# A gated mix of a spectral filter and a GEGLU network, forward and backward: the forward transform by six column classes, and another order at the start of pass two

## The chip, the core and the metric

One core of a Trainium2 chip runs the whole kernel in one launch. The time is the device time of an execution in microseconds (us). Engine names are those of the profile: PE is TensorE (PEld its weight loads), DVE is VectorE, ACT is ScalarE, POOL is GpSimd, SP is SyncE, which issues most DMAs. A name with a q (ACTq, POOLq) is an engine's own DMA issuing.

## The reference

With S = 2048 rows, D = 576 columns and F = 4608, everything in bfloat16 at the borders:

```python
g = sigmoid((x * gate_w).sum(-1, keepdims=True))
a = irfft2(rfft2(x) * (w_r + 1j * w_i))          # spectral filter, 2048 x 576
b = (gelu(x @ w_gate) * (x @ w_up)) @ w_down     # GEGLU network
out = g * a + (1 - g) * b
```

The kernel returns `out` and, for a given `grad_out`, the gradients of x, w_r, w_i, w_gate, w_up, w_down and gate_w (the B branch's own x enters as a constant, and both branches read A's x). So there are two forward transforms, one of x and one of g times grad_out, and two inverse ones: one gives a, the other the branch's part of the gradient of x.

## The kernel before

All matrix work is on TensorE in bfloat16, and the kernel has two passes.

**Pass one** (0 to about 919 us) loops over 18 column groups g of 256 columns of F, and in each over four stages m of 512 rows: 72 stages, counted by `pr`, some 12 us each. A stage computes `H_mm` (matmuls z, L490 and L495, and xy, L499 and L506), the activation and its derivative on ScalarE (`H_act`, L525 to L528, `H_da`, L518) and VectorE (`H_ew1`, L533 to L537; `H_ew2`, L553 to L574), and the weight gradients of the group before (`W_units`: dw_down at L618, dw_gate and dw_up at L636, a tail at L650). ScalarE or VectorE evicts those (L587) into staging tiles, which GpSimd's DMA queue stores (L628, L643). The tile q, written by ScalarE at L525, is read by VectorE through L570 of the same stage.

Between the W jobs of a stage stand pieces of the spectral work, the list `fft`. `want(pr)` says how many are to be done by stage pr: the first nine values are in `FIRST`, the rest grow evenly. `fft_next` emits the next piece; a piece marked `noslot` goes along with the next one and takes no slot. First come the forward transforms, 16 row tiles of x and then 16 of grad_out, from 73.7 to 356 us. A row tile has two pieces:

- `u1(t)`: matmuls from the transposed input (`xT`, `dOT`) along the columns, which are split in four classes of 128 columns and a tail of 64. Six matmuls: four of 146 columns out with the table `D4` (L679), two of 292 with the tail table `D4t` (L682). ScalarE evicts the result to Y (for grad_out with the scale `gs32`, which is g times a constant).
- `u2(t)`: two matmuls of 292 columns (L697) with the row table `Rt[t]`, an eviction on ScalarE (L701, 128x584 elements), and five VectorE operations (L702 to L709) that make the 289 frequencies out of 73; then a store to DRAM.

PSUM for the results of both pieces comes from the pool of z, which has one buffer. After 356 us come the pieces in the middle (transform along the rows, products with the spectral weights, gradients of w_r and w_i) to about 806 us.

**Pass two** (from about 919 us) multiplies the stored activations by the weights again: a list of jobs g0, g1, b0, ..., whose matmuls stand at L1194. The inverse transforms run between them as pieces: `z_piece` (six matmuls of 128 columns, L1244, evicted by ScalarE at L1246) and `d_piece` (six of 96 columns, L1254), released by a counter, `ticks`, which every block of twelve matmuls moves on. The inverse already works by six classes of columns: `fold` (L1221 to L1237, 17 VectorE operations) makes them out of the loaded frequencies Vp (`load_p`, L1210, on ScalarE's DMA queue). Ahead of the jobs `build_RT` (VectorE L215 to L221, ScalarE's sines at L222) and `build_I` (VectorE L181 to L204, a sine at L203) make the inverse's tables. `spread_gw` broadcasts gate_w over the partitions by two matmuls into two accumulators and two VectorE copies (L1186). Accumulators come from one pool in turn, so each use waits until the use some tiles before has been read. In every job some loads of the transposed w_up (`load_wuT`, nine pairs) go to SyncE's queue.

Instructions are issued on each engine in program order, and the program order is that in which the Python code calls them.

Of the kernel before, what the change touches and what calls it, by code (L numbers as in the profile page):

```python
# [9 lines left out]
ACT = mybir.ActivationFunctionType  # L10
# [28 lines left out]
QF = 73  # L39
# [23 lines left out]
def iotas(nc, res, unit):  # L63
    tb = Tables()
    G, V = nc.gpsimd, nc.vector
    kw = dict(allow_small_or_imprecise_dtypes=True)
    tb.halfpi = res.tile([P, 1], F32, name="halfpi")
    V.memset(tb.halfpi[:], math.pi / 2)
    tb.pi = res.tile([P, 1], F32, name="pi")
    V.memset(tb.pi[:], math.pi * EPS_SCALE)  # L70
    tb.warm = res.tile([P, 1], F32, name="warm")
    nc.scalar.activation(tb.warm[:], tb.halfpi[:], ACT.Sin)
    tb.lrow = unit([QF], F32, name="lrow")
    G.iota(tb.lrow[:], pattern=[[1, QF]], base=0, channel_multiplier=0, **kw)
    tb.dcol = res.tile([P, 5], F32, name="dcol")
    G.iota(tb.dcol[:, 0:4], pattern=[[1, 4]], base=0, channel_multiplier=4, **kw)
    for r in (LO, HI):
        G.iota(tb.dcol[r, 4:5], pattern=[[0, 1]], base=512, channel_multiplier=1, **kw)
    tb.dn = res.tile([P, 5], F32, name="dn")
    V.tensor_scalar(tb.dn[:], tb.dcol[:], 1.0 / D, None, op0=ALU.mult)  # L80
    tb.late = []
    tb.Dt = []
    tb.Rt = []
    return tb


def iotas_R(nc, tb, res, unit, kscr):
# [16 lines left out]
    r4_i = res.tile([P, 1], I32, name="r4_i")  # L104
    tb.r4 = res.tile([P, 5], F32, name="r4_f")

    def parity():
        V.tensor_single_scalar(par_i[:], tb.qcol_i[:], 1, op=ALU.bitwise_and)
        V.tensor_copy(tb.par[:, 1:2], par_i[:])
        V.tensor_scalar(tb.par[:, 0:1], tb.par[:, 1:2], -1.0, 1.0, op0=ALU.mult, op1=ALU.add)  # L110
        V.tensor_scalar(tb.kadd[:, 0, 1:2], tb.par[:, 1:2], float(S // 2), float(S // 4), op0=ALU.mult, op1=ALU.add)
        kr = unit([3, P], F32, name="kr")
        G.tensor_scalar(kr[0:1, 0, :], kk[0:1, 0, :], 16.0, None, op0=ALU.mult)
        G.memset(kr[0:1, 0, 1:2], float(S // 2))
        G.tensor_copy(kr[0:1, 1:3, :], kk[0:1])
        nc.sync.dma_start(kscr[:].rearrange("(o k) m -> o k m", o=1), kr[0:1])
        nc.sync.dma_start(tb.kc[:], kscr[:].rearrange("k m -> m k"))
        V.tensor_single_scalar(r4_i[:], tb.qcol_i[:], 3, op=ALU.bitwise_and)
        V.tensor_copy(tb.r4[:, 4:5], r4_i[:])
        for r in range(4):  # L120
            G.tensor_scalar(tb.r4[:, r:r + 1], tb.r4[:, 4:5], float(r), None, op0=ALU.is_equal)
# [8 lines left out]
def build_D(nc, tb, unit, c0, n, w):  # L130

    V, G = nc.vector, nc.gpsimd
    step = 2.0 * math.pi / D
    TS = (G if c0 else V).tensor_scalar
    X = unit([n, w], F32, name="XD")
    y = unit([n, w], F32, name="yD")
    for c in range(n):
        TS(y[:, c, :], tb.lrow[:, 0:w], tb.dn[:, c0 + c:c0 + c + 1], MAGIC, op0=ALU.mult, op1=ALU.add)
    TS(y[:], y[:], -MAGIC, -float(D), op0=ALU.add, op1=ALU.mult)
    o = unit([n, 2, w], name="Dt")  # L140

    def angles():
        for c in range(n):
            V.scalar_tensor_tensor(X[:, c, :], tb.lrow[:, 0:w], tb.dcol[:, c0 + c:c0 + c + 1], y[:, c, :],
                                   op0=ALU.mult, op1=ALU.add)
        V.scalar_tensor_tensor(y[:], X[:], -1.0, X[:], op0=ALU.mult, op1=ALU.max)

    def sines():
        if c0 == 0:
            v = o[:].rearrange("p (o r) c l -> p o (r c) l", o=2)  # L150
            co, si = v[:, :, 0:4:3, :], v[:, :, 1:3, :]
            yv, Xv = (t[:].rearrange("p (o r) l -> p o r l", o=2) for t in (y, X))
        else:
            co, si, yv, Xv = o[:, :, 0, :], o[:, :, 1, :], y[:], X[:]
        nc.scalar.activation(co, yv, ACT.Sin, bias=tb.halfpi[:], scale=-step)
        nc.scalar.activation(si, Xv, ACT.Sin, scale=-step * EPS_SCALE)
        if c0 == 0:
            tb.D4 = o

    def tails():  # L160
        tl = tb.D4t = unit([2, 2, 4, w], name="Dt")
        G.memset(tl[HI, 0], 0.0)
        G.memset(tl[LO, 1], 0.0)
        for k, h in enumerate((LO, HI)):
            for r in range(4):
                for c in range(2):
                    b = 3 * c if r % 2 == 0 else 2 - c
                    G.tensor_scalar(tl[h, k, r // 2, b], o[h, 0, c], tb.r4[h, r:r + 1], None, op0=ALU.mult)
    return angles, sines, tails


# [153 lines left out]
def kernel(  # L325
# [101 lines left out]
    gs32 = res.tile([P, T], F32, name="gs32")  # L427
# [243 lines left out]
    def fwd_units(src, dst, scale, ps=pftile):  # L671
        ys = {}

        def u1(t):
            def f():
                yps = ps()
                for o in range(2):
                    for r, bs in ((2 * o, slice(0, 4, 3)), (2 * o + 1, slice(1, 3))):
                        nc.tensor.matmul(yps[:, o, 0:4 * QF].rearrange("p (b l) -> p b l", b=4)[:, bs, :], lhsT=src[:, r, t, :],  # L679
                                         rhs=tb.D4[:, r], start=(r % 2 == 0), stop=False)  # L680
                for o in range(2):
                    nc.tensor.matmul(yps[:, o, 0:4 * QF], lhsT=src[:, 4, t, :],  # L682
                                     rhs=tb.D4t[:, t % 2, o].rearrange("p b l -> p (b l)"), start=False, stop=True)
                ys[t] = unit([2, 4 * QF], name="Y")
                if scale is None:
                    nc.scalar.copy(ys[t][:], yps[:, :, 0:4 * QF])
                else:
                    nc.scalar.activation(ys[t][:], yps[:, :, 0:4 * QF], ACT.Copy, scale=scale[:, t:t + 1])
            return f

        def u2(t):
            def f():
                Y = ys.pop(t)
                R = tb.Rt[t]
                vps = ps()
                for o in range(2):
                    nc.tensor.matmul(vps[:, o, 0:4 * QF], lhsT=R, rhs=Y[:, o], start=True, stop=True)  # L697
                Vt = half([2, DF], name="Vt")
                ve = unit([8, QF], F32, name="ve")
                M = unit([2, 2, 2, QF], F32, name="vm")  # L700
                nc.scalar.copy(ve[:].rearrange("p (o b) l -> p o (b l)", o=2), vps[:, :, 0:4 * QF])  # L701
                V.tensor_tensor(M[:, 0].rearrange("p u v l -> p v u l"), ve[:, 0:4].rearrange("p (v u) l -> p v u l", u=2),  # L702
                                ve[:, 4:8].rearrange("p (v u) l -> p v u l", u=2), op=ALU.add)
                V.tensor_tensor(M[:, 1, 0], ve[:, 0:2], ve[:, 4:6], op=ALU.subtract)
                V.tensor_tensor(M[:, 1, 1], ve[:, 6:2:-3], ve[:, 2:8:5], op=ALU.subtract)
                up = Vt[:, :, 0:DF - 1].rearrange("p c (k l) -> p k c l", k=2)[:, :, :, 0:QF]
                dn = Vt[:, :, DF - 1:0:-1].rearrange("p c (k l) -> p k c l", k=2)[:, :, :, 0:QF - 1]
                V.tensor_tensor(up, M[:, :, :, 0], M[:, :, :, 1], op=ALU.add)
                V.tensor_tensor(dn, M[:, :, :, 0, 0:QF - 1], M[:, :, :, 1, 0:QF - 1], op=ALU.subtract)  # L709
                LD.dma_start(dst[:, t], Vt[:])  # L710
            return f
        return [u1(t) for t in range(T)], [u2(t) for t in range(T)]

# [160 lines left out]
    D0 = build_D(nc, tb, unit, 0, 4, QF)  # L874
    D0[0]()
# [3 lines left out]
    D4 = build_D(nc, tb, unit, 4, 1, QF)  # L879
    for f in titems(wdn, wts[0][1][:].rearrange("p k (c m) -> p k c m", c=2), 0, (phtile, pgtile, phtile), (VC, AC, VC), n=2):  # L880
        f()
    D0[1]()
# [3 lines left out]
    D4[0]()  # L886
    D4[1]()
# [10 lines left out]
    fg = zipped(*fwd_units(xT, scr_x, None)) + zipped(*fwd_units(dOT, scr_g, gs32))  # L898
# [28 lines left out]
    FIRST = (0, 0, 0, 0, 0, 0, 1, 4, 7)  # L927
# [37 lines left out]
    for g in range(NG):  # L965
# [3 lines left out]
        for m in range(NPR):  # L969
# [15 lines left out]
            if g == 0:  # L985
# [37 lines left out]
                elif m == 1:  # L1023
                    next(makeB)
                    D4[2]()
                if m < NPR - 1:
                    gate(m + 1)
                else:
                    V.tensor_copy(g32[:], g_bf[:])
                    V.tensor_scalar(gs32[:], g32[:], SD2, None, op0=ALU.mult)  # L1030
# [5 lines left out]
            else:  # L1036
# [23 lines left out]
                if pr == 4:  # L1060
                    scale_dB(1, VC)
                elif pr == 5:
# [94 lines left out]
    with tc.tile_pool(name="p2f", bufs=3, **kw) as p2f, \  # L1157
# [44 lines left out]
        build_RT(nc, tb, f32t, RT)  # L1202
        build_I(nc, tb, f32t, lambda shape: p2s.tile([P] + shape, F32, tag="icol", name="icol", bufs=1), It)
# [7 lines left out]

# [65 lines left out]
        for i in range(2):  # L1277
            for w in range(2):
                load_p(i, w)
        for w in range(2):  # L1280
            fold(0, w)
        ticks = [0, 2]
# [113 lines left out]
        for i, (kind, t) in enumerate(jobs):  # L1396
            if i > 0 and wT_loads:
                load_wuT(*wT_loads.pop(0))
            if i == 1:
                spread_gw()  # L1400
# [45 lines left out]
```

## Time and profile before

| | |
|---|---|
| median of three runs | 1376.17 us (1375.54 to 1377.75) |
| the profiled execution | 1375.8 us, its span 1374.0 us, granted clock 0.997 |
| TensorE busy | 1354.6 us, 99% |
| VectorE busy | 844.1 us, 61% |
| ScalarE busy | 751.6 us, 55% |
| GpSimd busy | 259.8 us, 19% |
| DMA | 211.85 MB moved, mean 154 GB/s |

The page's slices (40 of equal length, each digit the busy share in tenths; PEclk is the granted TensorE clock):

```profile
PE   9999999999999999999999999998999999999998
DVE  7886766776658786786687655625535543545320
ACT  7886767766767776776777676621333322223210
PEclk9999999999999999999999999999999999999999
```

Pass two begins in slice 27 of 40 (each is 34.35 us long). A row of the profile names line, engine, operation, the tile written and the tile read, and its shape; times are from the start of the span. Matmuls are pipelined: a row's length includes the drain of the array, and rows overlap. A wait row reads "engine tile line <- engine tile line that released it: us in total, times, longest".

### The profile page before, as it was taken

To read this page: it belongs to the slowest core of one execution; us is meant where nothing else is said; L and a number is where in the kernel's file an instruction comes from. 1 tells how busy PE (TensorE), PEld (TensorE's weight loads), DVE (VectorE), ACT (ScalarE), POOL (GpSimd) and SP (SyncE) were. 2 spreads that over 40 slices of the span, in tenths; PEclk is the share of its full clock that TensorE was granted. 3 is DMA by queue.
4 is the path that set the end of the run, shared out by engine and by line. 5 is a ranking of instruction groups with operands and counts; after the bars stand their busy time and mean duration, and the time that the engine had idled before them with its cause. 6 is when DMAs were issued, how large, how long until landed. Compare 5 with 4: busy or idle time off the path is not lost.

```text
span 1374.0 us, 26478 instructions
## 1 busy us (share of the span) xinstructions
PE 1354.6 (99%) x10199; PEld 905.7 (66%) x10280; DVE 844.1 (61%) x1976; ACT 751.6 (55%) x1360; POOL 259.8 (19%) x508
## 2 busy tenths in 40 slices
PE   9999999999999999999999999998999999999998
PEld 7566656656655656655655665566888888888886
DVE  7886766776658786786687655625535543545320
ACT  7886767766767776776777676621333322223210
POOL 5210110111314432442441311100000000000000
PEclk9999999999999999999999999999999999999999
DMA  7435435435644754754664657499999888779773
GB/s 231 135 88 142 136 97 146 122 108 150 166 115 121 191 133 129 189 136 134 173 148 127 167 155 170 110 284 191 202 217 182 171 171 157 166 157 172 158 147 73
DMA packets 497397, 211.85 MB, mean 154 GB/s; under 512 B 307219, under 2 KB 488150, under 8 KB 497270
## 3 DMA queue, kind: packets, MB, share of 16 engines
q1 hardware_dynamic: 470932, 175.30, 55.3%
q0 software_dynamic: 14912, 24.24, 6.2%
q10 hardware_dynamic: 11426, 10.61, 3.4%
q8 instruction: 80, 1.31, 0.4%
q14 instruction: 47, 0.39, 0.1%
HBM read 43.13 MB, written 93.56 MB: 99 GB/s over the span
## 4 chain that ended last, share of the span: by engine, by line
PE 94%; DVE 2%; DMA 1%; issue 1%; ACT 1%; SPq 0%; ACTq 0%; POOL 0%; DVEq 0%; POOLq 0%
PE acc L1194 30%; PE xy L506 17%; PE wps L636 17%; PE wps L618 10%; PE z L490 9%; PE wps L650 2%; PE xy L499 2%; PE z L495 2%; DMA wd_all<-in_B_w_down_dram 1%; PE acc L1244 1%; PE pf L679 1%; PE acc L1254 1%; PE pf L697 1%; PE pf L682 1%; PE pf L839 1%
## 5 line engine op out<-in xcount | busy, mean ns | idle before, releaser
L1194 PEld LDWEIGHTS <-pin 128*128 128x128 bf16 x3456 | 336.0, 98 | 84.0 <-issue 0.3
L506 PE MATMUL xy<-wgu,xT 128*128 128x512 bf16 x1086 | 258.7, 379 | 8.5 <-issue 7.5
L636 PE MATMUL wps<-dH,xn 128*128 128x512 bf16 x1137 | 264.9, 379 | 0.9
L636 PEld LDWEIGHTS <-xn 128*128 128x128 bf16 x1152 | 112.5, 98 | 126.5 <-issue 0.6
L506 PEld LDWEIGHTS <-xT 128*128 128x128 bf16 x1152 | 106.8, 98 | 133.1 <-issue 24.8
L643 POOL DMA_DIRECT2D out_dram<-dw x134 | 72.9, 547 | 416.6 <-ACT dw L587 399.1
L618 PE MATMUL wps<-dB,A 128*128 128x288 bf16 x1152 | 149.6, 286 | 0.0
L1194 PE MATMUL acc<-wd_all,pin 128*128 128x288 bf16 x1152 | 148.9, 289 | 0.0
L1194 PE MATMUL acc<-wgT,pin 128*128 128x288 bf16 x1152 | 147.0, 286 | 0.0
L1194 PE MATMUL acc<-wuT,pin 128*128 128x288 bf16 x1152 | 146.0, 286 | 0.0
L1256 ACT ACTIVATE yo<-acc 128x288 bf16<-128x288 f32 x64 | 67.4, 1247 | 129.2 <-PE acc L1254 106.4
L490 PE MATMUL z<-wdT,dOT 128*128 128x256 bf16 x1152 | 137.7, 273 | 0.1
L618 PEld LDWEIGHTS <-A 128*128 128x128 bf16 x1152 | 112.7, 98 | 34.1
L518 ACT ACTIVATE da<-z,omg 128x256 bf16<-128x256 f32 x288 | 112.1, 472 | 34.5 <-PE z L495 34.4
L490 PEld LDWEIGHTS <-dOT 128*128 128x128 bf16 x1152 | 112.4, 98 | 21.7 <-DVE dOT L462 0.3
L1375 DVE TENSOR_TENSOR b16t<-acc,f32t 128x288 bf16<-128x288 f32 x32 | 14.7, 458 | 175.9 <-PE acc L1194 175.9
L527 ACT CAST xb<-xy 128x512 bf16<-128x512 f32 x144 | 85.3, 592 | 48.5 <-PE xy L506 48.5
L525 ACT ACTIVATE q<-xy 128x512 bf16<-128x512 f32 x144 | 88.4, 616 | 4.9 <-PE xy L506 3.4
L564 DVE TENSOR_TENSOR xb<-xb,sg 128x1024 bf16<-128x1024 bf16 x48 | 33.1, 690 | 94.3 <-ACT sg L556 94.3
L1246 ACT CAST Z<-acc 98x384 bf16<-98x384 f32 x64 | 27.5, 481 | 113.5 <-PE acc L1244 113.5
L528 ACT CAST hu<-xy 128x512 bf16<-128x512 f32 x144 | 87.6, 608 | 0.0
L587 ACT CAST dw<-wps 128x512 bf16<-128x512 f32 x72 | 42.3, 589 | 67.0 <-PE wps L636 66.0
(523 smaller groups left out, 1741.2 us busy)
## 6 DMA issues: line engine op xcount, KB each, us to landing
scr<-dH SPq DMA_DIRECT2D x144, 256.0 KB, 3.6
scr<-A SPq DMA_DIRECT2D x72, 256.0 KB, 2.7
out_dram<-dw POOLq DMA_DIRECT2D x134, 64.0 KB, 2.3
wd_all<-in_B_w_down_dram SPq DMA_DIRECT2D x3, 1728.0 KB, 10.4
out_dram<-dwd POOLq DMA_DIRECT2D x34, 144.0 KB, 3.0
scr_p<-Vt SPq DMA_DIRECT2D x32, 144.5 KB, 2.6
Vp<-scr_p ACTq DMA_DIRECT2D x32, 144.5 KB, 4.3
wgu<-in_B_w_gate_dram SPq DMA_DIRECT2D x18, 256.0 KB, 4.3
```

Of the source, the lines that this page charges most:

```text
L490: nc.tensor.matmul(zo(t), lhsT=dOT[:, ci, t, :], rhs=wdT[:, ci, :], start=(t % 4 < 2 and ci == 0), stop=False)
L506: nc.tensor.matmul(xy[k][:, t % 2, :], lhsT=xT[:, ci, t, :], rhs=wgu[:, ci, :], start=False, stop=(ci == 3))
L518: nc.scalar.activation(da[:, t, :], z[:, t % 2, t // 2, :], ACT.Copy, scale=omg32[:, 4 * m + t:4 * m + t + 1])
L525: nc.scalar.activation(q[:, h, :], xy[:, :, 0:FG], ACT.Square)
L527: nc.scalar.copy(xb[:, h, :], xy[:, :, 0:FG])
L528: nc.scalar.copy(hu[:, h, :], xy[:, :, FG:2 * FG])
L587: wcopy[0](out, in_)
L618: nc.tensor.matmul(wps[:, :288], lhsT=tl(0, t)[:, fch * P:(fch + 1) * P], rhs=dB[:, t, h * 288:(h + 1) * 288], start=(t == 0), stop=(t == ...
L636: nc.tensor.matmul(wps[:].rearrange("p a b -> p (a b)"), lhsT=xn[:, t, c * P:(c + 1) * P], rhs=kt[t // 4][1][:, t % 4].rearrange("p k f -> ...
L643: wst[0].dma_start(ov[:, c, fsl], dw[:, k, :])
L1194: nc.tensor.matmul(acc[:, :288], lhsT=src[:, r, :], rhs=w_of(r)[:, h * 288:(h + 1) * 288], start=(first and r == 0), stop=(last and r == F ...
L1256: nc.scalar.activation(yv[:, 3 * b:3 * b + 3], ps[:, 0:288].rearrange("p (r q) -> p r q", r=3), ACT.Copy, scale=(SD2, 1.0)[w])
```

## The change

1. **Six classes on the way in.** `build_D` with its tables `D4` and `D4t` gives way to `build_F`, one table `Ft` of six classes with 49 frequencies each. `u1` now takes the untransposed row tile, sorted by class (six groups of 96 columns), as the stationary operand and `Rt[t]` as the moving one: six matmuls with 96 rows and 128 columns out. `u2` takes six matmuls of 98 columns out with `Ft`, evicts 128x588, and makes the 289 frequencies with 17 VectorE operations.
2. **The sorting.** GpSimd copies x by class two row tiles at a time (`sort_x`, 8 copies of 128x1152 elements, strided reads), and grad_out one row tile at a time, times g (`sort_g`, 16 of 128x576), from a raw copy that SyncE's queue loads again (`load_g`, 8 of 288 KB). They are `noslot` pieces, five or six pieces ahead of the `u1` that reads them; the first is emitted in stage 4.
3. **FIRST** changes from (..., 0, 1, 4, 7) to (..., 0, 0, 3, 7).
4. **The start of pass two.** The first four `load_p` and `spread_gw` stand ahead of `build_RT` and `build_I`; the first piece comes at tick 4 instead of 2; `load_wuT` starts at the fourth job instead of the second.

The diff, cut to its core:

```diff
-    D0 = build_D(nc, tb, unit, 0, 4, QF)
-    D0[0]()
+    F0 = build_F(nc, tb, unit)
...
         def u1(t):
             def f():
-                yps = ps()
-                for o in range(2):
-                    for r, bs in ((2 * o, slice(0, 4, 3)), (2 * o + 1, slice(1, 3))):
-                        nc.tensor.matmul(yps[:, o, 0:4 * QF].rearrange("p (b l) -> p b l", b=4)[:, bs, :], lhsT=src[:, r, t, :],
-                                         rhs=tb.D4[:, r], start=(r % 2 == 0), stop=False)
-                for o in range(2):
-                    nc.tensor.matmul(yps[:, o, 0:4 * QF], lhsT=src[:, 4, t, :],
-                                     rhs=tb.D4t[:, t % 2, o].rearrange("p b l -> p (b l)"), start=False, stop=True)
+                zps = pftile()
+                row = src.pop(t)
+                for k, r in enumerate(CLS):
+                    nc.tensor.matmul(zps[0:96, k // 3, k % 3 * P:(k % 3 + 1) * P], lhsT=row[:, r], rhs=tb.Rt[t], start=True, stop=True)
...
         def u2(t):
             def f():
-                for o in range(2):
-                    nc.tensor.matmul(vps[:, o, 0:4 * QF], lhsT=R, rhs=Y[:, o], start=True, stop=True)
+                for k in range(6):
+                    nc.tensor.matmul(vps[:, k // 3, k % 3 * w:(k % 3 + 1) * w], lhsT=Z[0:96, k // 3, k % 3 * P:(k % 3 + 1) * P],
+                                     rhs=tb.F[0:96, k].rearrange("p c l -> p (c l)"), start=True, stop=True)
...
-                V.tensor_tensor(M[:, 0].rearrange("p u v l -> p v u l"), ve[:, 0:4].rearrange("p (v u) l -> p v u l", u=2),
-                                ve[:, 4:8].rearrange("p (v u) l -> p v u l", u=2), op=ALU.add)
...
+                V.tensor_tensor(sd[:, 0], lo, hi, op=ALU.add)
+                V.tensor_tensor(sd[:, 1, :, 0], hi[:, :, 0], lo[:, :, 0], op=ALU.subtract)
...
+                for k, op in enumerate((ALU.add, ALU.subtract)):
+                    V.tensor_tensor(M[:, k], sd[:, 0, 0], sd[:, 0, 1], op=op)
+                    V.tensor_tensor(M[:, 4 + k, 1::-1], sd[:, 1, 0], sd[:, 1, 1], op=op)
...
+    def sort_x(k):
+        def f():
+            q = classes(xq, k)
+            nc.gpsimd.tensor_copy(q[:], xn[:, 2 * k:2 * k + 2, :].rearrange("p t (q r) -> p t r q", r=6))
+        return noslot(f)
...
+    def sort_g(t):
+        def f():
+            if t % 2 == 0:
+                classes(gq, t // 2)
+            nc.gpsimd.tensor_scalar(gq[t], graw[t // 2][:, t % 2].rearrange("p (q r) -> p r q", r=6), g32[:, t:t + 1], None, op0=ALU.mult)
+        return noslot(f)
...
-    FIRST = (0, 0, 0, 0, 0, 0, 1, 4, 7)
+    FIRST = (0, 0, 0, 0, 0, 0, 0, 3, 7)
...
-        build_RT(nc, tb, f32t, RT)
-        build_I(nc, tb, f32t, lambda shape: p2s.tile([P] + shape, F32, tag="icol", name="icol", bufs=1), It)
...
+        for i in range(2):
+            for w in range(2):
+                load_p(i, w)
+        spread_gw()
+        build_RT(nc, tb, f32t, RT)
+        build_I(nc, tb, f32t, lambda shape: p2s.tile([P] + shape, F32, tag="icol", name="icol", bufs=1), It)
...
-        ticks = [0, 2]
+        ticks = [0, 4]
...
-            if i > 0 and wT_loads:
+            if i > 2 and wT_loads:
                 load_wuT(*wT_loads.pop(0))
-            if i == 1:
-                spread_gw()
```

## The prediction

> **What bounds the kernel now.** I read the page's busy line and its chain first. These are the busy times, then the shares of the chain that ended last:
>
> ```profile
> PE 1354.6 (99%) x10199; PEld 905.7 (66%) x10280; DVE 844.1 (61%) x1976; ACT 751.6 (55%) x1360; POOL 259.8 (19%) x508
> PE 94%; DVE 2%; DMA 1%; issue 1%; ACT 1%; SPq 0%; ACTq 0%; POOL 0%; DVEq 0%; POOLq 0%
> ```
>
> TensorE sets the end almost everywhere: only its work or its waits can move the time, and other engines count once they make it wait. Next, TensorE's waits from 919 to 975 us (start of pass two), and the windows around the one row found (columns: stretch, length, PE, PEld, DVE, ACT, POOL busy, granted clock, DMA share, GB/s):
>
> ```profile
> PE acc L1244 <- DVE gwf L1186: 4.6, 1, 4.6
> ...
> 944.00:946.00 2.00, 0.94 (x8) 0.85 (x9) 1.97 (x8) 0.35 (x1) 0.00 (x0) 0.50 1.04 195
> 946.00:948.00 2.00, 2.00 (x10) 1.30 (x9) 2.00 (x13) 0.51 (x2) 0.00 (x0) 0.50 0.98 150
> 948.00:950.00 2.00, 2.00 (x10) 1.26 (x9) 2.00 (x13) 0.00 (x0) 0.00 (x0) 0.50 1.19 286
> 950.00:951.00 1.00, 1.00 (x8) 0.69 (x6) 1.00 (x6) 0.00 (x0) 0.00 (x0) 0.68 1.93 40
> ```
>
> TensorE stands still for 4.6 us, then works at half clock until about 950.3. Third, the stretch in which the forward transform's pieces run, 87 to 356 us, and VectorE's longest waits there:
>
> ```profile
> 87.00:356.00 269.00, 266.46 (x1863) 161.53 (x1887) 196.42 (x394) 191.07 (x354) 33.38 (x62) 1.00 0.45 125
> ...
> DVE xb L564 <- ACT sg L556: 21.7, 14, 3.0
> DVE s L533 <- ACT q L525: 18.6, 10, 2.9
> DVE vm L702 <- ACT ve L701: 17.4, 19, 1.6
> DVE xb L564 <- ACT s L553: 6.5, 5, 1.3
> ```
>
> TensorE is full; VectorE is 73% busy and idles some 64 us in waits for ScalarE.
>
> **1. TensorE's matmuls in the forward pieces.** Rows of matmuls include the drain of the pipeline, so I take start to start from the timeline (start, length):
>
> ```profile
> 226.20 0.43 PE L679 MATMUL pf<-Dt,dOT 128*128 128x146 bf16 x4
> 226.46 0.41 PE L682 MATMUL pf<-Dt,dOT 128*128 128x292 bf16 x2
> 226.71 1.02 PE L506 MATMUL xy<-wgu,xT 128*128 128x512 bf16 x4
> ...
> 229.30 0.41 PE L697 MATMUL pf<-Y,Rt 128*128 128x292 bf16 x2
> 229.55 0.81 PE L636 MATMUL wps<-dH,xn 128*128 128x512 bf16 x3
> ...
> 958.76 0.42 PE L1254 MATMUL acc<-It,Z 98*128 98x96 bf16 x6
> 959.02 0.53 PE L1194 MATMUL acc<-wd_all,pin 128*128 128x288 bf16 x3
> ...
> 969.57 0.50 PE L1244 MATMUL acc<-RTt,F 128*98 128x128 bf16 x6
> 969.90 0.53 PE L1194 MATMUL acc<-wd_all,pin 128*128 128x288 bf16 x3
> ```
>
> Now: u1 0.51 (226.20 to 226.71) and u2 0.25, 0.76 us a row tile. After: u1 is six matmuls of 128 columns, as L1244's six (0.33), and u2 six of 98, as L1254's six of 96 (0.26): 0.59. Saving 0.17 x 32 row tiles = **5.4 us**, on the path. The other end is by busy rows: now 6.8 + 6.8 + 6.6 + 6.6 + 13.2 = 40.0 us; after 16.3/192 = 85 ns x 192 + 13.4/192 = 70 ns x 192 = 29.7; saving 10.3. I keep 5.4, since starts have no drains in them.
>
> **2. The stall at pass two.** z_piece (L1244) reuses the accumulators of spread_gw, whose copies L1186 stand in VectorE's queue behind the tables and two folds; the first fold waited 5.08 us for Vp, whose loads stand on ScalarE's queue behind It's sine:
>
> ```profile
> 932.26 1.96 ACTq L1210 DMA_DIRECT2D Vp<-scr_p  x4
> ...
> 938.41 0.36 DVE L1221 TENSOR_TENSOR pm<-Vp 128x196 f32<-128x196 bf16 x1 [5.08 <-DMA Vp<-scr_p]
> ...
> 944.55 0.82 DVE L1186 COPY gwf<-acc 128x288 f32<-128x288 f32 x2
> ```
>
> With spread_gw ahead of the tables, its copies come at about 920. The 4.6 us go, and with them the half clock: 945.06 to 950.3 is 5.24 us at half speed, 2.6 lost. Together 7.2 us. The Trainium skill, "TensorE: Matmul & The Clock Gate", Part 1, says that an idle window of some 3.4 us halves the clock and as much busy time restores it; here 4.6 us idle brought 6.4 us of 0.50 in the windows, and without the row the rule would give 1.7 for my 2.6. New wait: spread_gw's matmuls now come first on TensorE, and the second accumulator waits for the last dW eviction (ACT L587, 919.49, 0.58 long; now hidden behind twelve matmuls): 0.65 us. **Net 6.6 us.**
>
> What is late next: the four Vp loads now stand ahead of RT's sines on ScalarE's queue, and a DMA issue that waits for a free lane holds the queue. By the lane order the third waits for the third wd_all load (issued 917.2, landing 10.4 us later by its row, about 928). So ScalarE's RT work (923.8 to 929.7) moves to some 929.5 to 935; VectorE's tables behind it end near 938.5, and fold (0,0), 3.0 us, near 941.6. TensorE gets to its first z_piece, at tick 4 instead of 2, near 943.9: **2.3 us of slack, costed at nothing**. If wd_all lands more than 2.3 us later, the excess comes back as a wait, and past a few us the half clock's 2.6 with it. The nine wuT loads start two jobs later; the ninth is issued near 1026, lands 5 to 10 us later and is needed near 1039: 3 us of cover at worst, nothing.
>
> **3. VectorE's bill.** u2 has five operations now; after, 17 small ones on as many elements. Now start to start: 0.37 + 0.22 + 0.35 + 0.49 + 0.38 = 1.81 us (L702 to L709, from 90.68). After: the inverse's fold (L1221 to L1237) has 17 operations of these sizes too, 938.41 to 941.42 = 3.01. That is 1.2 x 32 = +38 us: 196 + 38 = 235 us of a stage that shrinks to 264, 89%. Off the path while the 64 us of waits absorb it; late work shows first as ScalarE's q (L525) waiting for L570, with 1.5 to 2.8 us of slack in the stages I followed. A stage with two u2 runs 2.4 us late on VectorE less its own waits: about 0.7 at its end. Tightest is 87 to 100 us, where VectorE was busy 12.35 of 13 (95%) and TensorE lost nothing: **about 1 us lost there**; bounds 0 and 3.
>
> **4. The sorts on GpSimd.** sort_x, 8 of 128x1152 (strided), and sort_g, 16 of 128x576, five or six pieces ahead of use. No row has their shape. Low: L187's iota of 576 elements took 640 ns, 1.1 ns each: 1.3 and 0.64 us, 20 us in all. High, the nearest kind (TENSOR_SCALAR while VectorE is busy):
>
> ```profile
> L168 POOL TENSOR_SCALAR Dt<-Dt,r_f x16: 463/814/1307, 27.8 to 40.4; 64x73 bf16<-64x73 bf16 x16
> ```
>
> 814/73 = 11 ns an element: 12.8 and 6.4 us, 205 in all; GpSimd had 33 of 269 us busy, so even that fits, but behind a 12.8 us sort the dW stores on its queue come too late for their staging (reused a stage later, 8 us of cover), some 5 us x 8. I take three times the low end, 3.8 and 1.9 us, 61 in all (a small L168 may be mostly fixed cost): no stall. What matters is whether a sort holds up VectorE. During L168's 13.44 us, VectorE's steps stood at 28.61, 29.07, 29.80, against 46.37, 46.84, 47.56 without it: unchanged, at most 0.2 us lost. The rule that speaks against the change is the Trainium skill, "SBUF — State Buffer", section "Who interferes with whom": a VectorE instruction with two SBUF inputs shuts out a GpSimd one that reads SBUF, or is shut out, whole instructions long. If only GpSimd waits, as L168's stretched rows suggest, it is free; by the rule at its worst every GpSimd microsecond is VectorE's loss. I take **0.5 us**; bounds 0 and the second rival.
>
> **5. The rest, at nothing.** D4 with its tails (12.8 us of GpSimd, 1.2 of VectorE and ScalarE) goes from the opening, where TensorE waits for loads and transposes. The eight grad_out loads (288 KB) on SyncE's queue wait for tiles long free; DMA there is 45% busy. ScalarE's Z eviction has 768 columns for 584: (655 − 481)/(584 − 384) = 0.87 ns each, 0.16 us x 32 = 5 us, 71 to 73% busy. Its one PSUM buffer had 0.9 us of slack. FIRST moves one piece from stage 6 to 8.
>
> **Sum.** −5.4 − 6.6 + 1 + 0.5 = −10.5; 1375.8 (profiled execution, span 1374.0) gives 1365.3; the median lies 0.37 higher: about **1365.5 us**.
>
> **Rivals.**
> (a) The stall at pass two returns: Vp or the sines land late, as 8.2 us for Vp's landing there hints. A lateness of 4 us past the slack, plus 2.6 of half clock, gives back 6.6: 1372. For it: DMA is saturated in those rows; against it: 2.3 us of slack. 0.14.
> (b) VectorE becomes the bound of 87 to 356 us because sorts shut it out for B us. At the 95% that the tightest stretch bore, the stage lasts (235 + B)/0.95: 247 for B = 0, 264 at B = 16, and B = 32 gives 281, +17 in place of the 1.5 of parts 3 and 4: 1381. Slower than before from about B = 28: my 61 us of sorts holding VectorE 46% of their time. For: it has 11% of room left; against: L168's row. 0.14.
> (c) The matmuls save by the busy rows, or the stages' stalls shrink too: −10.3 for −5.4, 1360.5. 0.12.
> (d) The change moves nothing (saving eaten by VectorE's extra 38 us in many stages, the stall back): about 1376. 0.06.
> Forecast itself: 0.54.
>
> A measurement of this kernel tells about 0.2%, 2.75 us, from no change: faster means below 1373.4. Faster: forecast, (c), (a) but for its tail, a little of (b): 0.78. Same 0.07: most of (d), the middle of (b). Slower 0.15: the rest of (b), and sorts that hold up the stores. Range 1360 to 1379: (c) below; above (a), (d) and the mild half of (b); left out are the worse part of (b) and the stores. The forecast's own range is 1362 to 1369.
>
> **What would show it.** Right: six matmuls of the new u1 within 0.35 us and of u2 within 0.28; no row of TensorE waiting for gwf, clock 1.00 from 920 on; VectorE near 235 us in the forward stage with its waits for ScalarE shrunk. Wrong: TensorE waiting in the forward stage for xy tiles behind ScalarE's q, itself behind L570; VectorE rows longer while a sort runs; sorts over 5 us; a z_piece waiting for F; a wuT wait near 1039.

## The result, and the profile after

The changed kernel takes 1371.8 us (1371.3 to 1373.5, 7 runs) against 1376.1 of the kernel before on the same chip: a ratio of 0.9968, 95% interval 0.9956 to 0.9979. It is faster by 4.3 us where 10.6 were forecast, and lies inside the range. The profiled execution took 1371.81 us, its span is 1370.0.

Busy times and the chain that ended last, of the changed kernel's page:

```profile
PE 1358.1 (99%) x10408; PEld 904.1 (66%) x10408; DVE 911.7 (67%) x2349; ACT 752.1 (55%) x1358; POOL 299.4 (22%) x508
PE 76%; DVE 1%; issue 0%; ACT 0%; DVEq 0%
```

TensorE still sets the end (the chain's shares add up to 77% here, against nearly all of the span before; the page does not say where the rest went). VectorE has 68 us more of work and GpSimd 40.

**Pass two.** TensorE's only wait after 900 us, and the windows in which it stood still and was slow before (columns as in the prediction):

```profile
PE acc L1198 <- ACT dw L553: 0.4, 1, 0.4
```

```profile
940.00:945.00 5.00, 5.00 (x43) 4.00 (x41) 4.59 (x24) 0.68 (x1) 0.00 (x0) 1.00 1.12 222
945.00:950.00 5.00, 5.00 (x46) 4.09 (x45) 5.00 (x30) 1.26 (x3) 0.00 (x0) 1.00 1.03 172
```

The wait for gwf and the half clock are gone; what is left is the short wait for the last dW eviction (now L553).

**The forward pieces.** TensorE's timeline, start and length:

```profile
86.68 0.50 PE L646 MATMUL pf<-Rt,xq 128*96 128x128 bf16 x6
87.02 1.03 PE L472 MATMUL xy<-wgu,xT 128*128 128x512 bf16 x4
...
92.40 0.43 PE L660 MATMUL pf<-Ft,Z 96*128 96x98 bf16 x6
92.67 1.03 PE L602 MATMUL wps<-dH,xn 128*128 128x512 bf16 x4
```

From start to start u1 (L646) takes 0.34 us and u2 (L660) 0.27. Over all 32 row tiles the medians are 0.335 and 0.273 (before: 0.514 and 0.253).

**The forward stage.** The same window as before, and VectorE's waits in it:

```profile
87.00:356.00 269.00, 264.78 (x2015) 160.88 (x2013) 259.39 (x766) 192.08 (x351) 83.03 (x83) 1.00 0.47 131
```

```profile
DVE sd L668 <- ACT ve L666: 2.5, 2, 1.3
DVE s L500 <- ACT ve L666: 0.5, 1, 0.5
DVE s L499 <- ACT q L491: 0.2, 1, 0.2
```

TensorE's five longest waits up to 366 us, without those of its first 10 (the first row, at 36 us, lies in the opening and was 0.2 before):

```profile
PE pf L411 <- DVE dOT L418: 1.6, 1, 1.6
PE pf L646 <- ACT Z L649: 1.3, 1, 1.3
PE pf L660 <- ACT Z L651: 1.2, 2, 0.7
PE pf L660 <- ACT Z L649: 1.0, 2, 0.5
PE z L456 <- DVE BTtab L727: 0.7, 1, 0.7
```

ScalarE's waits for VectorE in the window, then its timeline ahead of TensorE's wait of 1.3 us for Z:

```profile
ACT q L491 <- DVE s L536: 10.2, 6, 3.1
ACT q L491 <- DVE sg L536: 1.5, 1, 1.5
...
88.91 0.60 ACT L491 ACTIVATE q<-xy 128x512 bf16<-128x512 f32 x1 [1.45 <-DVE sg L536]
89.40 0.79 ACT L649 CAST Z<-pf 96x768 bf16<-96x768 f32 x1
```

VectorE is 96% busy, and its 64 us of waits for ScalarE have shrunk to 3. It has become the late one: ScalarE's q (L491) now waits 11.7 us for it (before: no such wait), the Z eviction (L649) stands behind q on ScalarE, and TensorE waits for Z.

**Why VectorE is so full.** The sorts' own rows, and the timeline around three of them:

```profile
L720 POOL TENSOR_SCALAR xq<-graw,g 128x576 bf16<-128x576 bf16 x16 | 39.6, 2475 | 0.6
L707 POOL COPY xq<-xn 128x1152 bf16<-128x1152 bf16 x8 | 14.0, 1758 | 0.0
```

```profile
27.13 1.78 POOL L707 COPY xq<-xn 128x1152 bf16<-128x1152 bf16 x1
27.30 2.17 DVE L528 TENSOR_TENSOR dH<-da,xb 128x1024 bf16<-128x1024 bf16 x1
...
82.70 3.42 POOL L707 COPY xq<-xn 128x1152 bf16<-128x1152 bf16 x2
82.70 3.72 DVE L284 TENSOR_TENSOR Btab<-oB,msB 128x256 bf16<-128x256 f32 x1 [1.14 <-ACT oB L281]
...
104.24 1.77 POOL L707 COPY xq<-xn 128x1152 bf16<-128x1152 bf16 x1
103.91 2.28 DVE L669 TENSOR_TENSOR sd<-ve 128x147 f32<-128x147 f32 x1
```

L528 takes 0.69 us elsewhere, Btab's product took 0.43 before, L669 takes 0.30. Each of them ends 0.2 to 0.6 us after the sort that overlaps it (Btab's after two sorts in a row): the VectorE instruction stands still until the sort is over. So it is at all eight sorts of x, also where the VectorE row begins before the sort's (L669 by 0.33 us; start times on GpSimd are rough). A sort of grad_out holds for a part of its length only:

```profile
198.71 2.03 POOL L720 TENSOR_SCALAR xq<-graw,g 128x576 bf16<-128x576 bf16 x1
198.41 1.47 DVE L674 TENSOR_TENSOR vm<-sd 128x98 f32<-128x98 f32 x1
199.80 0.25 DVE L673 TENSOR_TENSOR vm<-sd 128x98 f32<-128x98 f32 x1
```

L674 ends 0.86 us before the sort, and what follows it has its usual length. At all 16 sorts of grad_out the held instruction ends 0.4 to 0.9 us before the sort does; it loses 0.7 to 1.2 us. At eight of them a TENSOR_SCALAR of 128x1024 behind it loses 0.4 more and ends 0.3 after the sort. Added up over the forward stage (each VectorE row's length less the lower quartile of its line and shape), VectorE lost 28.8 us to the 21 sorts there, which took 48.4 on GpSimd (all 24: 53.7). Two more holds lie outside that sum: 1.5 us in the opening and 3.3 at Btab.

### The profile page after: what moved, and what is told of

It reads as the page before. It is cut to its first block, busy times and chain, and to the rows that moved or that the text cites. A ratio compares the mean times of both kernels' runs of the same rounds, so it can differ in the third digit from the quotient of the medians.

```text
span 1370.0 us, 27201 instructions
## 1 busy us (share of the span) xinstructions
PE 1358.1 (99%) x10408; PEld 904.1 (66%) x10408; DVE 911.7 (67%) x2349; ACT 752.1 (55%) x1358; POOL 299.4 (22%) x508
## 4 chain that ended last, share of the span: by engine, by line
PE 76%; DVE 1%; issue 0%; ACT 0%; DVEq 0%
PE acc L1207 31%; PE wps L602 13%; PE xy L472 12%; PE wps L584 7%; PE z L456 6%; PE wps L616 2%; PE xy L465 1%; PE z L461 1%; PE acc L1260 1%; PE acc L1270 1%; PE pf L848 1%; PE pf L770 1%; PE pf L646 0%; PE pf L660 0%; DVE sd L668 0%
## 5 line engine op out<-in xcount | busy, mean ns | idle before, releaser
L472 PE MATMUL xy<-wgu,xT 128*128 128x512 bf16 x1152 | 270.7, 380 | 0.0
L456 PE MATMUL z<-wdT,dOT 128*128 128x256 bf16 x1152 | 137.7, 273 | 0.8 <-DVE BTtab L727 0.7
L456 PEld LDWEIGHTS <-dOT 128*128 128x128 bf16 x1152 | 112.4, 98 | 22.5 <-issue 1.0
L491 ACT ACTIVATE q<-xy 128x512 bf16<-128x512 f32 x144 | 88.0, 613 | 16.6 <-DVE s L536 10.2
L553 ACT CAST dw<-wps 128x512 bf16<-128x512 f32 x72 | 42.3, 589 | 63.9 <-PE wps L602 62.9
```

The costliest lines, as they stand in the source:

```text
L456: nc.tensor.matmul(zo(t), lhsT=dOT[:, ci, t, :], rhs=wdT[:, ci, :], start=(t % 4 < 2 and ci == 0), stop=False)
L472: nc.tensor.matmul(xy[k][:, t % 2, :], lhsT=xT[:, ci, t, :], rhs=wgu[:, ci, :], start=False, stop=(ci == 3))
L491: nc.scalar.activation(q[:, h, :], xy[:, :, 0:FG], ACT.Square)
L553: wcopy[0](out, in_)
```

## The experiments

Each ratio is against the kernel before on the same chip. Its median there was 1376.4 us for the kernels e1, e2, e3 and e5, 1377.6 for e4, e6, e7 and e8, 1379.0 for e9 and e10, and 1375.0 for e11. Tenths of a microsecond are therefore read from the starts of the stages in the traces, not from these times.

**The two halves apart.** Theory: the halves are independent and the forward half is a loss.

The kernel before, with the start of pass two alone:

```diff
-        build_RT(nc, tb, f32t, RT)
...
         def load_p(i, w):
...
+        for i in range(2):
+            for w in range(2):
+                load_p(i, w)
+        spread_gw()
+        build_RT(nc, tb, f32t, RT)
...
-        ticks = [0, 2]
+        ticks = [0, 4]
-            if i > 0 and wT_loads:
+            if i > 2 and wT_loads:
```

> The kernel before with the fourth part alone (loads of Vp and spread_gw ahead of the tables, first piece at tick 4, wuT loads two jobs later). By the traces the changed kernel came to pass two 3.3 us late and ended 4.0 us early, so this part should be worth 7.3 us: 1368.8 us (0.9947), with no row of TensorE waiting for gwf and the clock at 1.00 from 919 us on. The other reading, that the changed forward stage shifted DMA traffic and helped pass two, gives less than 5 us: over 1371.

Measured: 1369.2 us, ratio 0.9948 (0.9931 to 0.9965): 7.2 us less, with no wait for gwf and the clock at 1.00. And the change without that part:

> The changed kernel with the start of pass two as before: the six classes, the sorts and FIRST alone. If the two halves add up, it is slower than before by the 3.3 us that the changed kernel has lost by stage 71: 1379.4 us (1.0024), with the wait of 4.6 us for gwf back. If the halves act on each other, it lies over 1 us from that.

Measured: 1379.2 us, ratio 1.0015 (0.9999 to 1.0031), the wait for gwf back at 3.0 us, with another of 2.6 behind it. The halves add up, as far as this kernel's spread (1375.2 to 1381.2) can tell. The six classes with their sorts on GpSimd brought no time by themselves.

**Without the sorts.** Theory S says that the sorts hold VectorE and so TensorE, theory D that the 17 operations alone fill it.

```diff
-                row = src.pop(t)
+                row = src(t)
...
-                    nc.tensor.matmul(..., lhsT=row[:, r], rhs=tb.Rt[t], start=True, stop=True)
+                    nc.tensor.matmul(..., lhsT=row[:, r * 96:(r + 1) * 96], rhs=tb.Rt[t], start=True, stop=True)
...
-        early.setdefault(max(4 * k - 7, 0), []).append(sort_x(k))
...
-        early.setdefault(2 * T + 2 * t - 6, []).append(sort_g(t))
```

> The changed kernel without the sorts: u1 reads 96 neighbouring columns of x or of grad_out instead of a class, so a and its gradients are not computed; everything else stays, the 17 operations too. Theory S (the sorts hold VectorE, some 29 us in the forward stage, 3.3 at Btab and 1.5 in the opening, and this makes TensorE wait): the 1.4 us of the opening and at least 4.8 of the 6.3 us of stalls of the forward stage go, 1365.6 us (0.9924), VectorE near 230 us in 87 to 356. Theory D (the 17 operations fill VectorE, the sorts matter little): only the opening comes back, 1370.4 us, and the stalls for Z stay.

Measured: 1365.7 us, ratio 0.9922 (0.9903 to 0.9942). The window and VectorE's longest waits:

```profile
87.00:356.00 269.00, 266.04 (x2014) 163.19 (x2039) 236.52 (x780) 195.46 (x359) 33.51 (x62) 1.00 0.47 134
```

```profile
DVE s L499 <- ACT q L491: 12.6, 5, 2.6
DVE sd L668 <- ACT ve L666: 7.7, 9, 1.3
DVE xb L530 <- ACT sg L522: 5.5, 4, 1.4
```

VectorE stands at 236.5 us, and it waits for ScalarE again. S holds, D falls. Laid beside the changed kernel by the start of each stage's first z matmul (L456), the sorts cost TensorE:

| from stage to stage | added us | the sort there, and what it held |
|---|---|---|
| 2 to 3 | 1.5 | first of x, at 27 us; L528 |
| 7 to 8 | 1.3 | second and third of x; Btab |
| 9 to 10 | 1.2 | fourth of x, at 104 us; u2's L669 |
| 16 to 17, 20 to 21, 24 to 25 | 0.7, 0.8, 0.7 | sorts of grad_out |

That is 6.1 us (the other stages after the first: 0), as the times say (1371.8 − 1365.7). The last four sorts of x held VectorE 1.6 to 2.1 us each and cost TensorE nothing: there the stage had room.

**The sorts, but five operations.** Is it the lump of a hold, or the lump on top of a VectorE without room?

```diff
-                e, o = sd[:, 0, 2], sd[:, 1, 2]
...
-                    V.scalar_tensor_tensor(dn[:, :, c], M[:, 4:6, c, 1:LQ - 1], s_, M[:, 2:4, c, 1:LQ - 1], op0=ALU.mult, op1=op)
+                flat = [sd[:, s].rearrange("p k c l -> p (k c l)") for s in range(2)]
+                for c in range(2):
+                    V.tensor_tensor(Vt[:, c, 0:DF], flat[c][:, 0:DF], flat[1 - c][:, 0:DF], op=ALU.add)
```

> The changed kernel with five VectorE operations in u2 instead of 17 (three as now, two that write all of Vt; a and its gradients are not computed by it). The sorts stay. Theory S alone (each sort is a lump of 2 us that no stage has room for): the stalls stay, 1370.5 to 1371.8 us. Theory J (a sort's lump stalls TensorE only because the 17 operations have taken VectorE's room; the lumps of the opening, 1.5, and at Btab, 1.3, fall where there was none anyway): the stalls at stages 10, 17, 21 and 25 go, 3.4 us, and some of the 1.7 that stay without sorts: 1367 to 1368.4.

Measured: 1367.4 us, ratio 0.9938 (0.9921 to 0.9954). By stages, the losses of the opening (1.5) and of Btab (1.3) stay; those at stages 10, 17, 21 and 25 are gone, and so is the wait for BTtab. The sort at 104 us still held a VectorE instruction for 2.0 us too long, and it cost TensorE nothing. Theory J holds.

**What a hold depends on.** Two kernels of the same sorts, cut smaller, or read in order. First cut smaller (grad_out's sorts likewise, six operations for one):

```diff
-            nc.gpsimd.tensor_copy(q[:], xn[:, 2 * k:2 * k + 2, :].rearrange("p t (q r) -> p t r q", r=6))
+            v = xn[:, 2 * k:2 * k + 2, :].rearrange("p t (q r) -> p t r q", r=6)
+            for t in range(2):
+                for r in range(6):
+                    nc.gpsimd.tensor_copy(q[:, t, r], v[:, t, r])
```

> The changed kernel with each sort as single operations of one class and one row tile (96 elements a partition: 12 in place of one for x, 6 for one of g). H1: a sort shuts VectorE out for one instruction's length and VectorE gets in between, as L168's short operations let it: VectorE loses under 10 us instead of 29, and the time is 1366 to 1368. H2: what counts is GpSimd's time in all, however it is cut: VectorE loses 25 us or more, 1371 to 1373.

Measured: 1372.2 us over nine executions (1371.5 to 1374.7), ratio 0.9967 (0.9950 to 0.9983). The time is in H2's range, but neither theory fits. The short operations took GpSimd 122.6 us where the long ones took 53.6, and by the same measure VectorE lost 15.6 us in the forward stage instead of 28.8, and 6.0 more at Btab. Timeline around the two places, GpSimd and VectorE:

```profile
82.15 6.08 POOL L710 COPY xq<-xn 128x96 bf16<-128x96 bf16 x24
...
82.13 6.38 DVE L284 TENSOR_TENSOR Btab<-oB,msB 128x256 bf16<-128x256 f32 x1 [1.13 <-ACT oB L281]
...
107.82 3.42 POOL L710 COPY xq<-xn 128x96 bf16<-128x96 bf16 x12
...
108.24 0.37 DVE L673 TENSOR_TENSOR vm<-sd 128x98 f32<-128x98 f32 x1
108.53 0.37 DVE L674 TENSOR_TENSOR vm<-sd 128x98 f32<-128x98 f32 x1
```

Btab's product waited for 24 GpSimd instructions in a row. It is the only one: at 108 us VectorE's instructions run in turn with the copies, each 0.11 us longer than its usual 0.26, and from 20 to 366 us no other VectorE instruction was held for more than 0.2 us. That is H1's mechanism, and the stages with sorts of grad_out cost TensorE nothing here. Btab's hold alone is most of the kernel's loss, 5.4 us from stage 7 to 8: a wait of 4.0 us for Z, then matmuls at a granted clock of 0.54 and 0.61 (92 to 96 us). Why this one instruction did not get in between is not shown. And in order, in both kinds of sort:

```diff
...
-  .rearrange("p t (q r) -> p t r q", r=6)
+  .rearrange("p t (r q) -> p t r q", r=6)
...
```

> The changed kernel with each sort reading its elements in order instead of every sixth (same sizes; the columns are not sorted, so a and its gradients are not computed). If the stride makes the sorts long, they take under 1.2 us (x) and 1.5 us (g) instead of 1.76 and 2.48, VectorE loses 15 us or less and the time is near 1368. If the hold is that of any GpSimd copy of this size, nothing moves: 1371 to 1372.

Measured: 1367.1 us, ratio 0.9935 (0.9916 to 0.9955). An undisturbed copy of x took 1.155 us instead of 1.755, one of grad_out 1.73 instead of 2.02 (under 1.5 was expected). VectorE lost 19.5 us, more than expected, yet 4.4 of TensorE's 6.1 us went (by the stages' starts): Btab's hold, now 2.1 us, and those of grad_out cost 0.3 together, the one in the opening (0.8 us) and the one at 102 us (1.4) still cost 0.8 and 0.6. The Trainium skill, "GPSIMD Engine Reference", section "7. Performance pitfalls for Q7 kernels", charges half as much again per element once the step between elements read exceeds 8 bytes; the step here is 12, and the two rows stand at 1.52 to 1. Those of grad_out, which also multiply, stand at 1.17 to 1.

**Sorting elsewhere.** TensorE could read the classes itself, with g in Rt:

```diff
-                row = src.pop(t)
+                row = src(t).rearrange("p (q r) -> p r q", r=6)
+                rt = Rg.pop(t) if scale is not None else tb.Rt[t]
...
+            nc.scalar.activation(Rg[t], tb.Rt[t], ACT.Copy, scale=g32[:, t:t + 1])
```

> The whole computation without sorts: TensorE loads each class as weights straight from the row tile, every sixth column, and g scales the rows of Rt (ScalarE, 128x128 a tile, 16 times) instead of grad_out. Theory S with weight loads of a stride that cost TensorE nothing: as the kernel without sorts, 1365.6 us (0.9924), and 0 to 1 more for 5 us of ScalarE. If strided weight loads are slower and not hidden (a load of 96 columns over 0.1 us, 192 of them), u1 takes over 0.4 us from start to start instead of 0.335 and the time is over 1368.

Measured: 1377.0 us, ratio 1.0009 (1.0000 to 1.0019). The weight loads (of this kernel, then of the changed one):

```profile
L651 PEld LDWEIGHTS <-graw 128*96 128x96 bf16 x96 | 15.0, 223 | 1.7
```

```profile
L646 PEld LDWEIGHTS <-xq 128*96 128x96 bf16 x185 | 14.4, 123 | 7.7 <-issue 2.2
```

A load with the step takes 223 ns instead of 123, and u1 0.72 us from start to start instead of 0.335: 0.38 x 32 = 12.3 us, nearly all on the path (by the stages' starts 11.5 us more than without sorts). The rival won.

All sorts on ScalarE:

```diff
-            nc.gpsimd.tensor_copy(q[:], xn[:, 2 * k:2 * k + 2, :].rearrange("p t (q r) -> p t r q", r=6))
+            nc.scalar.copy(q[:], xn[:, 2 * k:2 * k + 2, :].rearrange("p t (q r) -> p t r q", r=6))
...
-            nc.gpsimd.tensor_scalar(gq[t], graw[t // 2][:, t % 2].rearrange("p (q r) -> p r q", r=6), g32[:, t:t + 1], None, op0=ALU.mult)
+            nc.scalar.activation(gq[t], graw[t // 2][:, t % 2].rearrange("p (q r) -> p r q", r=6), ACT.Copy, scale=g32[:, t:t + 1])
```

> The whole computation with all sorts as ScalarE copies (8 of 128x1152, 16 of 128x576 times g) at the same places in the program. Theory S: VectorE's operations keep their lengths, the time is that of the kernel without sorts, 1365.7 us, plus what ScalarE's extra 25 us or so cost: it would be about 217 of 264 us busy in the forward stage, in order, and each copy delays the evictions behind it by 0.8 to 1.5 us. With that hidden: 1365.7 to 1367 (0.9922 to 0.993). Rival: the copies delay q and the Z evictions, and TensorE waits as long as with the sorts on GpSimd: 1369 to 1373.

Measured: 1373.6 us, ratio 0.9974 (0.9961 to 0.9988). VectorE's rows have their usual lengths, but TensorE waits on ScalarE:

```profile
PE pf L660 <- ACT Z L649: 4.3, 5, 1.6
PE pf L646 <- ACT Z L649: 1.7, 1, 1.7
```

The rival was right, for one half: 7.6 of the 8 us are lost from stage 7 to 15, where the sorts of x (1.8 us each) stand ahead of Z. The first, in stage 4, cost nothing, and all 16 of grad_out 0.4.

**Each sort where there is room.**

```diff
+            (nc.scalar.copy, nc.scalar.copy, V.tensor_copy, V.tensor_copy, *[nc.gpsimd.tensor_copy] * 4)[k](
+                q[:], xn[:, 2 * k:2 * k + 2, :].rearrange("p t (q r) -> p t r q", r=6))
...
                 elif pr == 5:
+                    sort_x(1)()
...
                 if pr == 6:
+                    sort_x(2)()
                     next(makeB)
+                    sort_x(3)()
...
-            nc.gpsimd.tensor_scalar(gq[t], graw[t // 2][:, t % 2].rearrange("p (q r) -> p r q", r=6), g32[:, t:t + 1], None, op0=ALU.mult)
+            nc.scalar.activation(gq[t], graw[t // 2][:, t % 2].rearrange("p (q r) -> p r q", r=6), ACT.Copy, scale=g32[:, t:t + 1])
```

> The whole computation with each sort on the engine that has room at its place: the first two of x on ScalarE (stages 4 and 5), the next two on VectorE just before and after Btab's product in stage 6, the last four on GpSimd as in the change, all 16 of grad_out on ScalarE. By the runs so far the GpSimd sorts that cost TensorE time are the first (1.5 us), the two at Btab (1.3), the one at 104 us (1.2) and those of grad_out (2.2), while ScalarE's sorts of grad_out cost under 0.4 us in all. Theory J (a hold costs only where VectorE has no room): near the kernel without sorts, 1365.7 to 1367.2 us (0.9915 to 0.993). If ScalarE's first sorts or VectorE's own two make q late instead: 1368 to 1371.

Measured: 1367.9 us, ratio 0.9911 (0.9897 to 0.9926); its profiled execution took 1366.9. The two waits at Btab and at 104 us, those behind the sorts of grad_out and the one in the opening are gone. One is new, 1.0 us for an eviction behind ScalarE's second sort:

```profile
PE wps L616 <- ACT dwd L553: 1.0, 1, 1.0
```

Then the copy of BT on ScalarE (`V.tensor_copy(tb.BT...)` becomes `nc.scalar.copy`):

> As the kernel with the sorts placed, and the copy of BT out of PSUM (256 columns, one) on ScalarE instead of VectorE. TensorE waits 0.7 us for that copy with and without sorts on GpSimd, and not with five operations in u2, so it waits for VectorE's queue of u2 operations. ScalarE is about 60% busy there: the wait goes and 0.5 to 0.9 us with it. If the copy then stands behind a late eviction on ScalarE, nothing moves.

Measured: 1366.1 us, ratio 0.9899 (0.9883 to 0.9916). The wait is gone, worth 0.83 us by the stages' starts. Last, sort_x(1) on VectorE beside Btab:

> As the kernel before (sorts placed, BT's copy on ScalarE), with the second sort of x on VectorE too, beside Btab in stage 6, instead of on ScalarE in stage 5. There TensorE waited 1.0 us for a dW-down eviction that stood behind that sort on ScalarE. VectorE idled some 3 us around Btab in the first kernel, and a sort takes it 0.94: three fit. If so, the 1.0 us goes: 1365.0 us (0.989 to 0.990 of the kernel before the change). If the third copy makes Btab's followers late (ScalarE's q waiting for L536), the gain is eaten: 1366 or more.

Measured: 1365.4 us (1364.9 to 1365.6), ratio 0.9929 (0.9915 to 0.9942; the chip's kernel before was at 1375.0). Stage 6 to 7 lost 1.06 in the two kernels before this one and loses 0 here. This version computes everything. It is about 10 us faster than the kernel before, and about 6 faster than the changed one (spans of 1363.8 and 1370.0 us).

## Why the forecast was too large

- **TensorE's saving: right.** Forecast 0.17 us a tile and 5.4 in all, measured 0.767 − 0.608 = 0.16 and 5.1. Rival (c), the busy rows, is refuted: starts are what counts.
- **Pass two: right.** Forecast 6.6, measured 7.2 alone, and 7.2 in the changed kernel (3.25 us late at stage 71, 3.99 early at the end). The new wait was 0.4 for 0.65. ScalarE's queue stood 5.5 us in the Vp issues and its sines began at 932.7 instead of 929.5, mostly because the kernel came to pass two late: the first fold ended at 945.3 and the z_piece came at 947.1, 1.9 us of slack for the 2.3 forecast. In the kernel with this part alone, the fold ended at 941.4 and the z_piece came at 944.4, against 941.6 and 943.9 in the forecast. Rival (a) did not happen.
- **VectorE's own bill: right.** Forecast 235 us, measured 236.5 without sorts. The stalls that it causes were forecast at 1 and came to 1.7 (from stage 3 to 29 the kernel without sorts gains 3.4 of TensorE's 5.1): some 0.7 near 100 us, 1.0 at BTtab, a queue that the forecast had not followed.
- **The sorts: wrong, and this is the whole error.** Part 4 took 0.5 us; the runs show 6.1, and 1365.5 + 5.6 is within 1 us of the measured time. The sorts' lengths were not the fault (1.76 and 2.48 us where 3.8 and 1.9 were taken; that the sums agree, 61 for 53.7, is luck, one being too long and the other too short). The step that failed is reading L168's row as "only GpSimd waits". Its operations had 73 elements and lengthened no VectorE row by more than 0.05 us; a sort has 576 or 1152 and lengthened them by 0.7 to 2.1. That the length makes the difference is not isolated, but the sorts cut to 96 elements point to it: there 0.11 us in the median, and at most 0.2, outside Btab. The rule that was set aside there, the Trainium skill's "SBUF — State Buffer", section "Who interferes with whom", lets a VectorE instruction with two SBUF inputs and a GpSimd one that reads SBUF shut each other out, and the runs bear that out. The sorts of x held it for their whole length; those of grad_out let the held one go 0.4 to 0.9 us before their end. GpSimd waits too: the same sort of grad_out took 2.02 to 3.40 us.
- **Rival (b) had the mechanism and the size.** It priced VectorE losses B between 16 and 32 us, and B came to 28.8. Its path cost was too high: (235 + 28.8)/0.95 = 277.7 us of stage, 13.7 lost, where 6.1 were, 2.8 of these outside the stage (1.5 in the opening, 1.3 at Btab). VectorE ran at 96% with TensorE losing little more than its single late spots. An average fill is a poor price: four holds of 2 us each and most of grad_out's cost nothing, the others 0.7 to 1.5, by what room their own stage had.
- **A sort was also early.** sort_x(0) stands in stage 4 of the program and ran at 27 us, in stage 1: GpSimd had nothing else queued. The forecast placed it where the code did.

## What to carry to other kernels

Moving work to an idle GpSimd is not free of VectorE: ask for every long GpSimd operation which VectorE instruction will overlap it, and what room that stage has. A row with short operations says nothing of long ones. What engine a helper copy belongs on can change from stage to stage: here the same sort was free on ScalarE in stage 4, on VectorE beside Btab and on GpSimd after 120 us, and cost 1 us and more in the wrong place. Cutting a long operation into short ones eased all holds but one; that one, on the path, ate the gain.

## What the runs showed that was not expected

- Short GpSimd instructions that follow each other closely can hold a VectorE instruction as one long one does: 24 of them held Btab's product for 6.38 us. Elsewhere in the same run VectorE got in between, 0.11 us late each time; what makes the difference stays open.
- A step of 12 bytes has its price. GpSimd's copy of 128x1152 takes 1.755 us instead of 1.155; the same sort took 0.94 on VectorE and 1.79 to 1.87 on ScalarE (no run has these two read in order). A weight load of 96 columns takes 223 ns instead of 123, and was not hidden behind the matmuls of 128 columns: u1 took 0.72 us instead of 0.335.
- Cutting a GpSimd copy of 1152 elements into 12 of 96 makes it longer even where nothing disturbs it: 24 of them took 6.08 us, 3.0 for 12, where one long copy takes 1.76.
